# One kernel of sparse attention and an ELU layer, with its order of work written anew: PSUM pairs in neighbouring banks, no clamps on GpSimd, tile fills between the loads

## The chip, the cores and the metric

The kernel runs on one core of a Trainium2 chip. The metric is device time in microseconds (us), the median of three runs. A core has five engines that are used here: TensorE (PE in the rows, PEld for its weight loads), VectorE (DVE), ScalarE (ACT), GpSimd (POOL, which also issues most loads) and SyncE (SP, which issues stores and transposing DMAs). They run side by side, each in its own fixed order, and wait for each other through semaphores. PSUM is the memory that TensorE writes its results to; it has 8 banks of 512 f32 columns.

## The reference

Eight heads of attention over 8 batches of 576 tokens, then a feed-forward layer with ELU:

```python
def _attn_ref(q, k, v):                       # (8, 8, 576, 64)
    scores = scale * np.matmul(q, k.transpose(0, 1, 3, 2))
    rel = pos[:, None] - pos[None, :]
    mask_local = (rel >= 0) & (rel < 32)                              # heads 0 to 3
    mask_strided = (rel >= 0) & (pos[None, :] % 32 == pos[:, None] % 32)   # heads 4 to 7
    attn = softmax(where(mask, scores, -1e9))
    return np.matmul(attn, v)

x = attn_out.transpose(0, 2, 1, 3).reshape(4608, 512)
h = x @ w_in                                  # 512 x 2048
g = np.where(h > 0.0, h, np.exp(np.minimum(h, 0.0)) - 1.0)
return g @ w_out                              # 2048 x 512
```

## The kernel before

The tokens of each batch are taken in 8 strided classes, so that a strided head attends inside its class pairs and a local head inside 32 neighbours. A piece of attention work is named `bcy.u`: batch `b`, kind `c` (`s` strided, `l` local), half `y` of the four heads, half `u` of the queries; there are 8 such pieces in a batch and 64 in all. A piece runs through a chain: scores `S` (TensorE, L418), exponential `e` (ScalarE, L425), mask `m` (VectorE, L432 or L438), times v and sums `O` (TensorE, L481 or L488; L445 to L466 in batches 0 and 1), logarithm of the sums `n` and its negative exponential `r` (ScalarE, L516 and L522: the reciprocal), and the product `x` that writes the layer's input `xT` (VectorE, L547).

The feed-forward layer takes the 4608 tokens in 9 chunks of 512. For each chunk 16 blocks `L` (or `a` and `b`, its two halves) of 4 matmuls make h (L595), ScalarE exponentiates (`h`, L603), a clamp to `exp(h) - 1` at most 0 follows (`i` on VectorE, `j` on ScalarE, `p` on GpSimd: L612 and L610), and VectorE takes the maximum with h into `g` (`g`, L623). Then 16 parts `Z` of 4 matmuls (L629) make the output, four parts to each 128 rows, which ScalarE copies out of PSUM (`o`, L635) and SyncE stores (`t`, L647).

All PSUM is one tile `ps` of 8 banks. A token of the text `ORDER` names the banks it writes: `L.1.3.1` one bank, `S.2s0.0.27` a pair, here banks 2 and 7. A pair is read in one instruction, as a slice with a step:

```python
def banks(s):
    i, j = int(s[0]), int(s[1])
    return ps[:, i:j + 1:j - i, 0:W]
```

The order of all work is that text: the loop at the end calls a function for each token, and so each engine gets its instructions in the order of the tokens. The layer below it sets the semaphore waits from the tiles and slices that instructions read and write.

Batches 0 and 1 are transposed by TensorE (`T`, L382 and L385). From batch 2 on, GpSimd loads q, k and v (`Ls`, `Ll`: L238, L245, L252, L262, L264), SyncE transposes them by DMA (`Ts`, `Tl`: L574, L577, L580) and copies the keys into zero-padded tiles `kps` and `kpl` (`Ks`, `Kl`: L588). The 8 spare rows of the tiles that are transposed are filled once from q (L563), inside `load_str` of batch 2. The padded tiles and the constant blocks of the v tiles are filled by GpSimd (L325 to L333), after all loads of the list `LOADS`. A run of `w` tokens is TensorE multiplying zeros (L363).

Of the kernel before, what the change touches and what calls it, by code (L numbers as in the profile page):

```python
# [46 lines left out]
n.0l0.0 m.0l1.0 O.0l1.1.67 r.0l0.0 n.0l0.1 O.0l1.0.23 x.0l0.0 r.0l0.1 a.0.0.0 n.0l1.0 x.0l0.1
a.0.1.1 r.0l1.0 a.0.2.4 n.0l1.1 x.0l1.0 a.0.3.5 r.0l1.1 a.0.4.2 x.0l1.1 a.0.5.3 b.0.0 b.0.1
h.0.0 b.0.2 h.0.1 b.0.3 i.0.0 g.0.0 b.0.4 h.0.3 b.0.5 i.0.1 h.0.4 a.0.6.6 i.0.3 g.0.1 b.0.6
h.0.5 a.0.7.7 g.0.3 h.0.2 b.0.7 j.0.5 a.0.8.0 i.0.2 i.0.4 a.0.9.1 h.0.6 g.0.4 b.0.8 h.0.7 g.0.5  # L50
a.0.10.5 j.0.7 a.0.11.2 g.0.2 a.0.12.3 h.0.8 g.0.7 b.0.9 j.0.6 b.0.10 i.0.8 h.0.9 g.0.6 b.0.11
h.0.10 b.0.12 g.0.8 a.0.13.4 h.0.12 i.0.10 a.0.14.7 g.0.10 h.0.11 Ll.2 b.0.13 b.0.14 i.0.12
# [60 lines left out]
L.5.2.4 i.5.0 h.5.1 g.5.0 O.6s0.0.15 i.5.1 h.5.2 L.5.3.2 g.5.1 n.6s0.0 i.5.2 L.5.4.7 r.6s0.0
g.5.2 Kl.6 Ll.7 O.6s0.1.03 h.5.3 x.6s0.0 Z.4.0.3.6 n.6s0.1 i.5.3 S.6s1.0.14 g.5.3 r.6s0.1
# [43 lines left out]
def kernel(  # L158
# [162 lines left out]
    for nm in LOADS:  # L321
        load(nm)
# [374 lines left out]
```

## Time and profile before

| | |
|---|---|
| three runs | 404.1, 404.48, 406.24 us, median 404.48 |
| the profiled execution | 405.33 us, of which the span is 403.4 |
| busy share of PE, DVE, ACT, POOL | 79%, 59%, 57%, 26% |
| mean granted TensorE clock | 0.961 of full speed |
| DMA moved | 40.59 MB, mean 101 GB/s |

The span is cut in stages by what TensorE does: until 20.6 us the attention of batch 0; until 80 the layer's chunk 0, the attention of batch 1 and the first loads for batch 2; until 332 the attention of batches 2 to 7, with blocks `L` and parts `Z` between; and from there the rest of the layer alone. The views give busy times per engine, and for idle time the instruction whose end released the one that waited.

### The profile page before, as it was taken

To read this page: it belongs to the slowest core of one execution; us is meant where nothing else is said; L and a number is where in the kernel's file an instruction comes from. 1 tells how busy PE (TensorE), PEld (TensorE's weight loads), DVE (VectorE), ACT (ScalarE), POOL (GpSimd) and SP (SyncE) were. 2 spreads that over 40 slices of the span, in tenths; PEclk is the share of its full clock that TensorE was granted. 3 is DMA by queue.
4 is the path that set the end of the run, shared out by engine and by line. 5 is a ranking of instruction groups with operands and counts; after the bars stand their busy time and mean duration, and the time that the engine had idled before them with its cause. 6 is when DMAs were issued, how large, how long until landed. Compare 5 with 4: busy or idle time off the path is not lost.

```text
span 403.4 us, 6126 instructions
## 1 busy us (share of the span) xinstructions
PE 319.4 (79%) x2263; PEld 161.2 (40%) x2302; DVE 237.0 (59%) x431; ACT 228.0 (57%) x388; POOL 106.2 (26%) x135
## 2 busy tenths in 40 slices
PE   6896788675778777778577686878988789999995
PEld 5643434332334343344233343434444334444442
DVE  3779835366416866665447665777467649639300
ACT  3785464464546775657556565676667756346121
POOL 8639932155000670432361205200000000000000
PEclk9999598899958999999999999999999999999999
DMA  8999996959714894898199819931421110110132
GB/s 151 189 206 189 132 159 130 156 63 175 117 26 120 125 132 80 137 150 143 49 117 134 165 41 144 83 89 51 99 72 28 26 28 0 48 58 0 53 80 79
DMA packets 110214, 40.59 MB, mean 101 GB/s; under 512 B 91784, under 2 KB 103752, under 8 KB 110184
## 3 DMA queue, kind: packets, MB, share of 16 engines
q0 software_dynamic: 71376, 18.75, 46.6%
q1 hardware_dynamic: 38808, 21.44, 22.8%
q8 instruction: 18, 0.29, 0.3%
q14 instruction: 12, 0.10, 0.1%
HBM read 38.03 MB, written 9.44 MB: 118 GB/s over the span
## 4 chain that ended last, share of the span: by engine, by line
PE 52%; DVE 18%; ACT 15%; DMA 8%; issue 4%; POOL 2%; SPq 0%; ACTq 0%; DVEq 0%; POOLq 0%
PE ps L629 24%; PE ps L595 21%; DVE xT L547 7%; ACT ln L516 6%; DVE g L623 5%; DVE he L612 5%; ACT e L425 4%; PE ps L418 4%; ACT he L603 2%; DMA kl<-in_k_dram 2%; ACT rc L522 2%; DMA kps<-kTs 2%; DMA qTs<-qs 2%; DMA ks<-in_k_dram 1%; PE ps L488 1%
## 5 line engine op out<-in xcount | busy, mean ns | idle before, releaser
L629 PE MATMUL ps<-w_out_sb,g 128*128 128x512 bf16 x557 | 143.6, 390 | 20.5 <-DVE xT L547 8.6
L595 PE MATMUL ps<-xT,w_in_sb 128*128 128x512 bf16 x556 | 137.5, 383 | 16.5 <-DVE xT L547 6.3
L603 ACT ACTIVATE he<-ps 128x512 f32<-128x512 f32 x144 | 84.4, 597 | 46.7 <-PE ps L595 36.0
L623 DVE TENSOR_TENSOR g<-he,ps 128x512 bf16<-128x512 bf16 x136 | 93.2, 687 | 21.7 <-ACT ln L516 7.3
L629 PEld LDWEIGHTS <-g 128*128 128x128 bf16 x576 | 54.4, 100 | 81.9 <-issue 30.7
L595 PEld LDWEIGHTS <-w_in_sb 128*128 128x128 bf16 x576 | 54.8, 98 | 79.7 <-issue 22.8
L612 DVE TENSOR_SCALAR he<-he 128x512 bf16<-128x512 f32 x130 | 64.0, 494 | 29.8 <-ACT he L603 29.4
L547 DVE TENSOR_TENSOR xT<-ps,rc 64x576 bf16<-64x576 f32 (+1 forms) x64 | 43.4, 680 | 62.9 <-ACT e L425 15.8
L425 ACT ACTIVATE e<-ps 72x576 bf16<-72x576 f32 (+1 forms) x64 | 40.9, 647 | 33.5 <-PE ps L418 13.7
L516 ACT ACTIVATE ln<-ps 64x576 f32<-64x576 f32 (+1 forms) x64 | 37.4, 584 | 38.0 <-PE ps L629 10.7
L635 ACT COPY osb<-ps 128x512 f32<-128x512 f32 x36 | 21.1, 585 | 40.1 <-PE ps L629 36.5
L522 ACT ACTIVATE rc<-ln 64x576 f32<-64x576 f32 (+1 forms) x64 | 39.7, 621 | 2.0
L245 POOL DMA_DIRECT2D ql<-in_q_dram x24 | 20.1, 845 | 46.5 <-DMA qTl<-ql 46.5
L612 POOL TENSOR_SCALAR he<-he 128x512 bf16<-128x512 f32 x6 | 12.0, 2004 | 48.8 <-ACT he L603 48.8
L418 PE MATMUL ps<-qTs,kps 128*128 128x72 bf16 x192 | 10.6, 198 | 15.7 <-DVE xT L547 5.7
L252 POOL DMA_DIRECT2D kl<-in_k_dram x24 | 18.1, 786 | 0.0
L432 DVE TENSOR_TENSOR pm<-e,mask_s 72x576 bf16<-72x576 bf16 x32 | 14.5, 461 | 5.9 <-ACT e L425 5.3
L438 DVE TENSOR_TENSOR pm<-e,mask_l 128x576 bf16<-128x576 bf16 x32 | 14.4, 454 | 5.9 <-ACT e L425 5.2
L418 PEld LDWEIGHTS <-kps 128*128 128x128 bf16 x192 | 9.1, 99 | 21.6 <-issue 18.8
L481 PE MATMUL ps<-pm,vsp 72*128 72x72 bf16 x192 | 11.0, 201 | 5.2 <-DVE xT L547 1.6
L481 PEld LDWEIGHTS <-vsp 72*128 72x128 bf16 x192 | 9.9, 101 | 12.6 <-issue 7.4
L418 PE MATMUL ps<-qTl,kpl 128*128 128x96 bf16 x144 | 10.3, 211 | 5.4 <-ACT ln L516 4.1
(87 smaller groups left out, 174.1 us busy)
## 6 DMA issues: line engine op xcount, KB each, us to landing
out_dram<-osb SPq DMA_DIRECT2D x32, 144.0 KB
vl<-in_v_dram POOLq DMA_DIRECT2D x8, 288.0 KB, 6.5
w_in_sb<-in_moe_w_in_dram POOLq DMA_DIRECT2D x4, 512.0 KB, 10.3
w_out_sb<-in_moe_w_out_dram POOLq DMA_DIRECT2D x4, 512.0 KB, 14.8
vs<-in_v_dram POOLq DMA_DIRECT2D x7, 288.0 KB, 7.7
kps<-kTs SPq DMA_DIRECT2D x12, 160.0 KB
ql<-in_q_dram POOLq DMA_DIRECT2D x24, 72.0 KB, 3.5
kl<-in_k_dram POOLq DMA_DIRECT2D x24, 72.0 KB, 3.7
```

The costliest lines, as they stand in the source:

```text
L418: nc.tensor.matmul(dst, lhsT=kt[pr, k0:k0 + 128], rhs=rhs, start=True, stop=True, skip_group_check=True)
L425: nc.scalar.activation(e[0:R], tiles.pop(("S", key, u))[0:R], ACT.Exp, scale=scale)
L481: nc.tensor.matmul(ov[:, x, j * RS:(j + 1) * RS], lhsT=vs_p[:, c0:c0 + 128], rhs=pm[0:RS, z, n0:n0 + RS], start=True, stop=True, skip_grou ...
L516: nc.scalar.activation(t, s_ps, ACT.Ln)
L522: nc.scalar.activation(t, tiles.pop(("ln", key, u)), ACT.Exp, scale=-1.0)
L547: nc.vector.tensor_mul(dst, o_ps, rc)
L595: nc.tensor.matmul(tiles["h", ch, m], lhsT=w_in_sb[:, c, m * 128:(m + 1) * 128], rhs=xT[:, c, ch * CHUNK:(ch + 1) * CHUNK], start=(c == 2) ...
L603: nc.scalar.activation(e, tiles["h", i[0], i[1]], ACT.Exp)
L612: eng.tensor_scalar(e1, e, scalar1=1.0, scalar2=1.0, op0=ALU.min, op1=ALU.subtract)
L623: nc.vector.tensor_tensor(dst, e1, h, op=ALU.max)
L629: nc.tensor.matmul(ops, lhsT=g[ch % 2][:, m, kk * 128:(kk + 1) * 128], rhs=w_out_sb[:, m, :], start=(m == 0), stop=(m == MC - 1), skip_gro ...
L635: nc.scalar.copy(o_sb, tiles.pop(("o", int(ch), int(kk))))
```

## The change

There are four edits. Every token of `ORDER` is placed anew, and its pairs are now all neighbours (01, 12, ... 67); the code that reads them is unchanged. The new text has no `p` token: the 6 clamps on GpSimd are gone, `j` has 9 in place of 8, and VectorE has 135 clamps in place of 130. There are 68 zero matmuls `w` in place of 30. The fills of padded tiles and constant blocks are cut in seven, and one stands after each load from the fifth of `LOADS` on. The fill of spare rows moves out of `load_str` of batch 2 to a place after the load `wi3`, ahead of `wo0`.

```diff
 ORDER = """
-w.7.28 K.q.1 K.q.0 K.k.1 K.k.0 T.0s0.q.0 c.0s0.q T.0s0.k.1 T.0s1.q.2 c.0s0.k T.0s1.k.3 C.0s1.q
...
+w.7.42 K.q.0 K.q.1 T.0s0.q.0 K.k.0 w.7.5 C.0s0.q T.0s1.q.1 K.k.1 w.7.2 T.0s1.k.0 C.0s1.q w.7.1
...
-    for nm in LOADS:
-        load(nm)
-
-    for (c, z), t in kp.items():
+    def fill_kp(c, z):
+        t = kp[c, z]
         nc.gpsimd.memset(t[(1 - z) * D:(2 - z) * D, :], 0.0)
-        if c == "s":
-            nc.gpsimd.memset(t[z * D:(z + 1) * D, 2 * NS * RP:], 0.0)
-        else:
-            nc.gpsimd.memset(t[z * D:(z + 1) * D, 0:PRE], 0.0)
-    for t, n in ((vl_t[0], HG * LB), (vl_t[1], HG * LB), (vs_p, HG * NS)):
+        s_ = slice(2 * NS * RP, None) if c == "s" else slice(0, PRE)
+        nc.gpsimd.memset(t[z * D:(z + 1) * D, s_], 0.0)
+
+    def fill_ones(t, n):
         nc.gpsimd.memset(
             t[:, 0:2 * n * D].rearrange("p (n w d) -> p n w d", w=2, d=D)[:, :, 0, :], 1.0)
         nc.gpsimd.memset(t[:, 2 * n * D:], 1.0)
+
+    def fill_rows(nm, x):
+
+        nc.gpsimd.dma_start(
+            out=raw[nm][RS:RP].rearrange("p (h f) -> p h f", h=HG),
+            in_=x[0, 0:HG].rearrange("h (p s) d -> p h (s d)", s=NS)[0:RP - RS])
+
+    fills = [lambda cz=cz: fill_kp(*cz) for cz in kp]
+    fills += [lambda a=a: fill_ones(*a)
+              for a in ((vl_t[0], HG * LB), (vl_t[1], HG * LB), (vs_p, HG * NS))]
+    for i, nm in enumerate(LOADS):
+        load(nm)
+        if nm == "wi3":
+            for a in (("qs", q), ("ks", k), ("ql", q)):
+                fill_rows(*a)
+        elif i >= 4 and fills:
+            fills.pop(0)()
...
-        if int(b) == NPE:
-
-            for nm, x in (("qs", q), ("ks", k), ("ql", q)):
-                nc.gpsimd.dma_start(
-                    out=raw[nm][RS:RP].rearrange("p (h f) -> p h f", h=HG),
-                    in_=x[0, 0:HG].rearrange("h (p s) d -> p h (s d)", s=NS)[0:RP - RS])
```

Lines of the changed kernel that stand behind the text are named by its own numbers: `L` and `Z` are L603 and L637 there, `e`, `n`, `r` and `x` L439, L530, L536 and L561, and `h`, `o` L611 and L643.

The first place is GpSimd's queue in the load stage, ahead of the loads of batch 2 (`ql` and `kl` in the last rows). Before:

```order
L325 MEMSET kpl_109 64x1184
L329 MEMSET kpl_109 64x32
L331 MEMSET vl_99 128x24x64
L333 MEMSET vl_99 128x64
L331 MEMSET vl_100 128x24x64
L333 MEMSET vl_100 128x64
L331 MEMSET vsp 72x32x64
L333 MEMSET vsp 72x64
L245 DMA ql<-in_q_dram 72x8x64 x4
L252 DMA kl<-in_k_dram 96x6x64 x4
```

And now:

```order
L238 DMA g_88<-in_v_dram 72x4x512
L328 MEMSET vl_99 128x24x64
L330 MEMSET vl_99 128x64
L238 DMA xT<-in_q_dram 72x4x512
L328 MEMSET vl_100 128x24x64
L330 MEMSET vl_100 128x64
L238 DMA xT<-in_k_dram 72x4x512
L328 MEMSET vsp 72x32x64
L330 MEMSET vsp 72x64
L262 DMA vl_100<-in_v_dram 96x24x64
L275 DMA w_out_sb<-in_moe_w_out_dram 128x4x512 x2
L245 DMA ql<-in_q_dram 72x8x64 x4
```

The fourteen memsets of the seven fills no longer stand in one run between the last load of `LOADS` and the first of batch 2; at most two follow each other.

The second place is ScalarE's queue where batch 2 ends and batch 3 begins (`ln<-ps` twice is `n` of the pieces 2l1.0 and 2l1.1, in banks 1 and 5, and 3 and 6), with the semaphores that each row waits for. Before:

```order
L425 ACTIVATE e<-ps 128x576 [waits DVE_49,PE_49]
L425 ACTIVATE e<-ps 128x576 [waits DVE_49]
L635 COPY osb<-ps 128x512 [waits DMAHW5_49,DMAHW4_49,DMAHW3_49]
L425 ACTIVATE e<-ps 72x576 [waits DVE_49,PE_49]
L516 ACTIVATE ln<-ps 64x576 [waits PE_49] x2
L522 ACTIVATE rc<-ln 64x576 [waits Activation_49]
L522 ACTIVATE rc<-ln 64x576
L425 ACTIVATE e<-ps 72x576 [waits DVE_49]
```

And now, where the first `ln` is that of 2l1.1, in banks 3 and 4, and the second that of 2l1.0, in banks 0 and 1:

```order
L439 ACTIVATE e<-ps 128x576 [waits DVE_49,PE_49]
L536 ACTIVATE rc<-ln 64x576 [waits Activation_49]
L439 ACTIVATE e<-ps 72x576 [waits DVE_49,PE_49]
L530 ACTIVATE ln<-ps 64x576 [waits DVE_49]
L530 ACTIVATE ln<-ps 64x576 [waits PE_49,Activation_49]
L536 ACTIVATE rc<-ln 64x576 [waits Activation_49]
L536 ACTIVATE rc<-ln 64x576 [waits DVE_49]
L439 ACTIVATE e<-ps 72x576 [waits PE_49]
L643 COPY osb<-ps 128x512 [waits DMAHW7_49,DMAHW6_49,DMAHW5_49]
```

The work is nearly the same and in nearly the same order; what moved is which banks the waits are about. In the built program of before, the first of the two `ln` waits for part `Z.1.1.1.4` and the second for `Z.1.1.2.4`, both in bank 4, which neither reads; now the first waits for an earlier VectorE reader of its own bank 4, and the second for the matmuls into its own bank 1. Followed in this way through both built programs, from each wait's value to the instruction that raises the semaphore to it, 668 waits of before tie two instructions that both touch PSUM with a bank in common or with one lying between the other's two, and in 276 of them no bank is common; of those 276, 85 are waits of PE, 121 of ACT and 70 of DVE. In the changed program there are 671 such waits and every one has a bank in common. PE's own waits of this sort were 133 with a common bank and 85 without, and are now 238 and none.

The third place is GpSimd's queue in the middle of the program, where clamps stood ahead of the loads of a batch:

```order
-L612 TENSOR_SCALAR he_1611<-he 128x512
-L245 DMA ql<-in_q_dram 72x8x64 x4
-L252 DMA kl<-in_k_dram 96x6x64 x4
-L262 DMA vl_99<-in_v_dram 96x24x64
-L264 DMA vl_99<-in_v_dram 32x23x64
-L612 TENSOR_SCALAR he_1762<-he 128x512
```

The loads stay, in the same order among themselves; no clamp stands between them.

## Rows read from the trace of the kernel before

**Rows 1.** The page, part 1: busy time of the engines.
```profile
PE 319.4 (79%) x2263; PEld 161.2 (40%) x2302; DVE 237.0 (59%) x431; ACT 228.0 (57%) x388; POOL 106.2 (26%) x135
```
**Rows 2.** Stages: length; busy PE, PEld, DVE, ACT, POOL; PE's clock; DMA; GB/s.
```profile
0.00:20.60 20.60, 15.22 (x254) 12.74 (x255) 11.50 (x31) 12.26 (x24) 15.71 (x30) 1.00 1.16 171
20.60:80.00 59.40, 46.29 (x390) 23.72 (x397) 37.92 (x63) 33.37 (x66) 30.33 (x39) 0.86 1.24 163
80.00:332.00 252.00, 191.34 (x1318) 94.63 (x1342) 154.67 (x273) 156.25 (x256) 60.11 (x67) 0.97 0.69 96
332.00:403.40 71.40, 66.56 (x304) 30.14 (x308) 32.96 (x64) 26.14 (x44) 0.00 (x0) 1.00 0.16 45
```
**Rows 3.** What PE waited for: total us, times, longest.
```profile
PE ps L418 <- ACT ln L516: 9.5, 9, 2.0
PE ps L629 <- DVE xT L547: 8.6, 7, 2.1
PE ps L629 <- ACT e L425: 6.4, 9, 0.9
PE ps L595 <- DVE xT L547: 6.3, 8, 1.2
PE ps L418 <- DVE xT L547: 5.7, 5, 2.0
...
PE ps L595 <- ACT e L425: 4.3, 5, 1.1
PE ps L595 <- ACT ln L516: 4.2, 6, 1.5
PE ps L629 <- ACT ln L516: 3.7, 5, 0.7
```
**Rows 4.** Timeline, 113 to 122 us: start, length, instruction, idle time before it.
```profile
113.28 1.86 PE L629 MATMUL ps<-w_out_sb,g 128*128 128x512 bf16 x4 [0.73 <-ACT e L425]
115.18 0.64 ACT L516 ACTIVATE ln<-ps 64x576 f32<-64x576 f32 x1 [1.95 <-PE ps L629]
...
118.25 0.64 ACT L516 ACTIVATE ln<-ps 64x576 f32<-64x576 f32 x1 [2.43 <-PE ps L629]
...
118.94 3.57 PE L629 MATMUL ps<-w_out_sb,g 128*128 128x512 bf16 x8 [0.73 <-ACT ln L516]
...
120.92 1.44 DVE L547 TENSOR_TENSOR xT<-ps,rc 64x576 bf16<-64x576 f32 x2 [7.20 <-ACT e L425]
```
**Rows 5.** Timeline, 36.9 to 42.8 us: a clamp beside GpSimd's fills.
```profile
36.91 5.02 DVE L612 TENSOR_SCALAR he<-he 128x512 bf16<-128x512 f32 x1
...
36.95 1.38 POOL L331 MEMSET vl<- 128x1536 bf16 x1
...
39.76 1.80 POOL L331 MEMSET vsp<- 72x2048 bf16 x1
...
42.71 0.64 PE L382 MATMUL ps<-identity,xT 72*128 72x72 bf16 x8 [4.63 <-DVE g L623]
```
**Rows 6.** The same columns, after that stall and around rows 4.
```profile
42.70:51.00 8.30, 7.74 (x112) 4.97 (x113) 7.21 (x15) 5.14 (x10) 8.30 (x11) 0.50 1.53 110
110.00:125.00 15.00, 11.19 (x68) 5.11 (x67) 3.92 (x7) 7.35 (x12) 0.00 (x0) 0.66 0.18 38
```
**Rows 7.** Timeline, batch 2's loads: last row fill, first transpose, first scores.
```profile
53.05 0.64 POOL L563 DMA_DIRECT2D ql<-in_q_dram  x1
...
61.14 1.39 SPq L574 DMA_TRANSPOSE qTs<-qs  x1
...
74.07 0.19 PE L418 MATMUL ps<-qTs,kps 128*128 128x72 bf16 x1 [2.77 <-DMA kps<-kTs]
```
**Rows 8.** Groups by line: clamps on both engines, and the zero matmuls.
```profile
L612 DVE TENSOR_SCALAR he<-he 128x512 bf16<-128x512 f32 x130 | 64.0, 494 | 29.8 <-ACT he L603 29.4
L612 POOL TENSOR_SCALAR he<-he 128x512 bf16<-128x512 f32 x6 | 12.0, 2004 | 48.8 <-ACT he L603 48.8
L363 PE MATMUL ps<-zero 128*128 128x128 bf16 x30 | 3.8, 312 | 1.1 <-DVE zero L289 1.1
```

More of the change, by code (lines that the diff above doesn't have):

```diff
@@ L47 @@
[L47 to L52, printed above, removed]
@@ new lines @@
+S.0s1.1.23 T.0l0.q.4 e.0s1.0 m.0s0.1 e.0s1.1 O.0s0.0.56 c.0l0.q O.0s0.1.01 m.0s1.1 n.0s0.0
+T.0l1.q.7 m.0s1.0 r.0s0.0 n.0s0.1 x.0s0.0 T.0l0.k.4 r.0s0.1 C.0l1.q O.0s1.0.23 c.0l0.k
+O.0s1.1.56 n.0s1.0 x.0s0.1 T.0l1.k.7 r.0s1.0 V.0 n.0s1.1 S.0l0.0.01 x.0s1.0 r.0s1.1 w.4.2
+c.0l1.k e.0l0.0 S.0l0.1.23 w.4.4 x.0s1.1 e.0l0.1 m.0l0.0 S.0l1.1.01 S.0l1.0.45 m.0l0.1 e.0l1.1
+O.0l0.0.67 e.0l1.0 O.0l0.1.23 m.0l1.1 a.0.0.0 n.0l0.0 m.0l1.0 O.0l1.1.45 r.0l0.0 n.0l0.1 a.0.1.1
+x.0l0.0 r.0l0.1 O.0l1.0.67 n.0l1.1 x.0l0.1 r.0l1.1 a.0.2.2 n.0l1.0 x.0l1.1 a.0.3.3 r.0l1.0
@@ new lines @@
+T.1l0.q.3 i.0.15 g.0.15 S.1s0.0.12 i.0.14 T.1l1.q.5 e.1s0.0 g.0.14 T.1l0.k.7 c.1s1.k C.1l1.q
+c.1l0.q S.1s0.1.12 m.1s0.0 S.1s1.1.45 c.1l0.k e.1s0.1 T.1l1.k.3 e.1s1.1 m.1s0.1 O.1s0.0.12 V.1
+S.1s1.0.67 n.1s0.0 c.1l1.k O.1s0.1.45 e.1s1.0 m.1s1.1 Z.0.0.1.0 n.1s0.1 m.1s1.0 r.1s0.1
+O.1s1.1.67 r.1s0.0 x.1s0.1 Z.0.0.2.0 n.1s1.1 x.1s0.0 r.1s1.1 O.1s1.0.34 x.1s1.1 S.1l0.0.12
+n.1s1.0 Z.0.0.3.0 r.1s1.0 e.1l0.0 x.1s1.0 S.1l0.1.56 o.0.0 S.1l1.0.34 m.1l0.0 Z.0.1.0.7 e.1l0.1
+t.0.0 e.1l1.0 m.1l0.1 O.1l0.0.12 S.1l1.1.56 m.1l1.0 n.1l0.0 O.1l0.1.34 Ll.2 r.1l0.0 Ls.2
@@ new lines @@
+Z.0.3.0.3 e.2s0.1 x.2s0.0 e.2s1.0 m.2s0.1 S.2s1.1.45 Z.0.3.1.3 Ts.3 e.2s1.1 m.2s1.0 h.1.9
+O.2s0.1.12 m.2s1.1 O.2s1.0.67 L.1.10.4 n.2s0.1 i.1.9 g.1.9 r.2s0.1 Z.0.3.2.3 n.2s1.0 x.2s0.1
+Z.0.3.3.3 r.2s1.0 h.1.10 O.2s1.1.01 x.2s1.0 L.1.11.2 n.2s1.1 i.1.10 S.2l0.0.56 g.1.10 r.2s1.1
+L.1.12.7 e.2l0.0 x.2s1.1 L.1.13.4 Ks.3 o.0.3 m.2l0.0 h.1.11 W.3 S.2l0.1.56 O.2l0.0.01 t.0.3
+h.1.12 i.1.11 L.1.14.3 Ls.4 g.1.11 n.2l0.0 i.1.12 r.2l0.0 L.1.15.2 g.1.12 h.1.14 x.2l0.0
+Z.1.0.0.7 h.1.13 i.1.14 e.2l0.1 g.1.14 S.2l1.1.01 Z.1.0.1.7 e.2l1.1 m.2l0.1 i.1.13 h.1.15
@@ new lines @@
+m.2l1.1 O.2l0.1.56 S.2l1.0.01 g.1.13 n.2l0.1 Z.1.0.2.7 Tl.3 i.1.15 e.2l1.0 g.1.15 O.2l1.1.34
+r.2l0.1 m.2l1.0 S.3s0.0.01 Z.1.0.3.7 e.3s0.0 x.2l0.1 n.2l1.1 m.3s0.0 O.2l1.0.01 S.3s1.0.56
+n.2l1.0 Z.1.1.0.2 r.2l1.0 Z.1.1.1.2 r.2l1.1 x.2l1.0 Z.1.1.2.2 e.3s1.0 x.2l1.1 o.1.0 O.3s0.0.01
+m.3s1.0 n.3s0.0 Kl.3 Ll.4 L.2.0.3 r.3s0.0 L.2.1.7 t.1.0 h.2.0 x.3s0.0 L.2.2.4 h.2.1 i.2.0 g.2.0
+S.3s0.1.56 h.2.2 O.3s1.0.01 i.2.1 L.2.3.3 e.3s0.1 i.2.2 g.2.2 n.3s1.0 L.2.4.5 g.2.1 h.2.3
+L.2.5.4 m.3s0.1 h.2.4 i.2.3 r.3s1.0 O.3s0.1.67 i.2.4 Z.1.1.3.2 g.2.3 n.3s0.1 g.2.4 L.2.6.3
@@ new lines @@
+S.7s1.0.45 i.6.3 L.6.4.6 e.7s1.0 g.6.3 O.7s0.1.12 m.7s1.0 h.6.4 Z.5.0.2.7 n.7s0.1 i.6.4
+O.7s1.0.34 g.6.4 L.6.5.0 r.7s0.1 n.7s1.0 x.7s0.1 S.7s1.1.56 Z.5.0.3.7 r.7s1.0 e.7s1.1 L.6.6.1
+x.7s1.0 h.6.5 m.7s1.1 S.7l0.0.56 Z.5.1.0.4 o.5.0 i.6.5 g.6.5 h.6.6 t.5.0 O.7s1.1.23 L.6.7.7
+e.7l0.0 i.6.6 g.6.6 n.7s1.1 S.7l0.1.56 m.7l0.0 Z.5.1.1.4 r.7s1.1 h.6.7 O.7l0.0.01 x.7s1.1
+Z.5.1.2.4 n.7l0.0 i.6.7 g.6.7 L.6.8.2 r.7l0.0 e.7l0.1 x.7l0.0 L.6.9.7 h.6.8 m.7l0.1 S.7l1.0.56
+h.6.9 i.6.8 O.7l0.1.01 g.6.8 e.7l1.0 L.6.10.3 i.6.9 n.7l0.1 g.6.9 Z.5.1.3.4 r.7l0.1 m.7l1.0
@@ new lines @@
+L.8.4.0 h.8.3 i.8.2 g.8.2 L.8.5.1 h.8.4 i.8.3 g.8.3 L.8.6.7 h.8.5 i.8.4 g.8.4 L.8.7.2 h.8.6
+i.8.5 L.8.8.0 g.8.5 h.8.7 i.8.6 L.8.9.3 g.8.6 h.8.8 i.8.7 L.8.10.1 h.8.9 g.8.7 L.8.11.7 i.8.8
+h.8.10 g.8.8 L.8.12.2 i.8.9 h.8.11 g.8.9 L.8.13.0 h.8.12 i.8.10 g.8.10 L.8.14.3 h.8.13 i.8.11
+g.8.11 L.8.15.1 h.8.14 i.8.12 Z.7.0.1.6 g.8.12 h.8.15 i.8.13 Z.7.0.2.6 g.8.13 i.8.14 Z.7.0.3.6
+g.8.14 i.8.15 Z.7.1.0.0 o.7.0 g.8.15 Z.7.1.1.0 t.7.0 Z.7.1.2.0 Z.7.1.3.0 Z.7.2.0.1 o.7.1
+Z.7.2.1.1 t.7.1 Z.7.2.2.1 Z.7.2.3.1 Z.7.3.0.0 o.7.2 Z.7.3.1.0 t.7.2 Z.7.3.2.0 Z.7.3.3.0
@@ L154 @@
+Z.8.0.0.1 o.7.3 Z.8.0.1.1 t.7.3 Z.8.0.2.1 Z.8.0.3.1 Z.8.1.0.0 o.8.0 Z.8.1.1.0 t.8.0 Z.8.1.2.0
+Z.8.1.3.0 Z.8.2.0.1 o.8.1 Z.8.2.1.1 t.8.1 Z.8.2.2.1 Z.8.2.3.1 Z.8.3.0.0 o.8.2 Z.8.3.1.0 t.8.2
+Z.8.3.2.0 Z.8.3.3.0 o.8.3 t.8.3
 """
```

179 lines of the change are left out of this document (73 added, 106 removed).

## The prediction

> **What bounds the kernel now.** The first view is the busy time of the engines [rows 1]: PE is the busiest at 319.4 us of a span of 403.4, so 84.0 us of the span are PE idle, and no other engine is over 59%. The span therefore ends where PE's work plus PE's idle time ends, and what I look for is what ended each idle stretch. The second view cuts the busy time by stage [rows 2]. Before 20.6 us PE idles 5.4, until 80 us 13.1, in the attention of batches 2 to 7 60.7, and in the rest 4.8. So nearly three quarters of the idle time lie in the third stage, where VectorE and ScalarE are busy 61% and 62% of it: nobody is full, and everybody waits. The same rows show a clock loss: at 0.86 in the second stage and 0.97 in the third, about 46.29 x 0.14 = 6.5 and 191.34 x 0.03 = 5.7 us of PE's time were lost to the lower of the two clock levels, 1.2 instead of 2.4 GHz.
>
> The third view is PE's waits [rows 3]. The eight longest that concern this change sum to 48.7 us, and they are odd: output parts (L629) and blocks of the first layer (L595) wait for an exponential, a logarithm or a write of `xT` in attention, with which they share no data. The fourth view is a timeline of one such place [rows 4]: a part L629 waits 0.73 us for `e`; then `ln` waits 1.95 for that part; the next `ln` waits 2.43 for the next part; PE waits 0.73 for that `ln`; `xT` sits idle 7.20. Two streams that share nothing run in turns instead of side by side. In the program these are the waits without a common bank that the second order excerpt shows: a pair with a step is treated as if it took all banks from its first to its last. The timeline gives their price, the program only their place.
>
> **Part by part.** The sum is made against the profiled execution, 405.3 us, which is 0.85 above the median of the three runs.
>
> Neighbouring pairs and the new order (term 1). All 276 waits without a common bank go. What of PE's idle time was theirs? I take each of the eight rows [rows 3] with the share of the program's waits between those two lines that have no common bank: L418 behind `ln` 9 of 12 of 9.5, L629 behind `xT` 8 of 8 of 8.6, L629 behind `e` 11 of 13 of 6.4, L595 behind `xT` 8 of 17 of 6.3, L418 behind `xT` 5 of 16 of 5.7, L595 behind `e` 9 of 12 of 4.3, L595 behind `ln` 7 of 12 of 4.2, L629 behind `ln` 7 of 7 of 3.7. That is 7.1 + 8.6 + 5.4 + 3.0 + 1.8 + 3.2 + 2.4 + 3.7 = 35.2 us, the upper bound. It is not all won, since behind each stands a true wait: PE has 105 more waits on a common bank than before (238 against 133), because neighbours must be free together and pairs such as 0 and 1 are used again at once. In before, 218 waits of PE on PSUM cost the 48.7 us, 0.22 each; 105 x 0.22 = 23 us would leave a gain of 12. But a part of that 0.22 was handed on: ScalarE and VectorE were themselves held by 191 waits of this kind, as the 1.95, 2.43 and 7.20 us show [rows 4]. I take half of the upper bound, **-17.6** (0.17 per new wait), and keep -35 and +10 as the ends; a loss cannot be excluded, as the rivals say.
>
> Fills between the loads (term 2). In before a clamp on VectorE, 0.49 us in the mean [rows 8], took 5.02 us, exactly while GpSimd ran its last six memsets back to back, and PE then sat 4.63 us [rows 5]. Cut in pieces of at most 1.80 us [rows 5] and parted by loads, the fills can no longer hold VectorE for so long; but they now stand earlier, and I work out from the order that four of the seven still meet the clamps of chunk 0. Between 0 and -4.6 I take **-3.0**, nearer the latter since the stall is a measured row. The Trainium skill, "SBUF — State Buffer", section "SBUF: two separate sides", says that VectorE in a two-port mode and GpSimd exclude each other, and that who starts first holds the shared ports for its whole instruction. By that rule alone the clamp would have waited for one memset, at most 1.80 us; the trace shows 5.02, so it does not agree on the length. By it the four fills could each hold a clamp again for their whole length, the term would be 0, and the time 378.
>
> Clock (term 3). After the 4.63 us of idleness PE ran 8.3 us at a granted clock of 0.50, and around rows 4 it ran 15 us at 0.66 [rows 6]: 7.74 x 0.50 = 3.9 and 11.19 x 0.34 = 3.8 us of slow work. Both follow from idle time that terms 1 and 2 remove. I take **-6.0**, ends 0 and -12 (all that is lost in rows 2).
>
> Row fills ahead of `wo0` (term 4). The last of the three was issued at 53.05, the first transpose of batch 2 could start at 61.14 only, and PE's first scores of batch 2 came at 74.07 after 2.77 us of waiting for the padded keys [rows 7]. Now no row fill follows batch 2's loads (3 x 0.64 us of issue), and GpSimd reaches those loads earlier. But the DMA engines move 163 GB/s over that stage with a share over 1 [rows 2], so the data comes little sooner. **-2.0**, ends 0 and -5. GpSimd's queue pays three issues earlier instead, with the loads of batch 1 behind them: 3 x 0.64 = 1.9 us at a point where its loads wait for the DMA engines anyway, so nothing; were that cover gone, 1.9.
>
> No clamps on GpSimd (term 5). One took 2004 ns, on VectorE 494 [rows 8], and GpSimd waited 48.8 us for their inputs with loads queued behind. Those loads were not late later on, so that wait costs nothing. Five more clamps add 5 x 0.49 = 2.5 us to VectorE, hidden in its 41% of idle time. The six chains shorten by 1.5 us each, of which I count one on the path: **-1.5**, ends -9 and +2.5.
>
> Zero matmuls (term 6). 38 more at 3.8 / 30 = 0.127 us [rows 8] are 4.8 us at most. They stand before the layer's first block, where PE idles 5.4 of 20.6 us. **+0.5**, ends 0 and 4.8.
>
> Stage four stays: PE is busy 66.56 of 71.4 us there [rows 2]; more or less work behind attention only shifts between stages.
>
> Sum: 405.3 - 17.6 - 3.0 - 6.0 - 2.0 - 1.5 + 0.5 = 375.7, against the median 374.9; I say **375**.
>
> **The rivals.**
> - *Nearly everything comes back.* If the new order is met as written, term 1 gives its whole 35, the clock 9, the rest -7: 405 - 51 = 354, with 5 more or less. For it speaks that VectorE and ScalarE have 38% of idle time in the third stage; against it, that PE's waits on PSUM grow in number, from 218 to 238.
> - *The waits move.* The 105 new waits cost the old 0.22 to 0.30 each: term 1 is -12 to -4, the clock gives 3, the fills 1, the rest 1: about 391, between 386 and 402. For it speaks that the order still has TensorE wait in line behind a reader of the bank that it writes next.
> - *Slower.* One mechanism: PE is blocked in order by a pair that isn't free. A block or part behind such a score waits too, though its own bank is free. The place is the third stage, where scores and `O` follow each other in the same pair. The price is 105 x p; the other terms without the clock are -6, so it decides from p = (35.2 + 6) / 105 = 0.39 us on, and at p = 0.45 the idle time that stays also keeps the clock low: 405 + 6 = 411. The longest single waits of that kind took 2.0 us [rows 3]; against it stands the mean of 0.22.
> - *No change that can be told.* The pace is set by loads, not by waits on PSUM: then 404. Against it: PE waited for padded keys 2.77 us at the first scores [rows 7], and no DMA is among the long rows of PE's waits [rows 3].
>
> **How the numbers follow.** The forecast (363 to 386) gets 0.54, nearly everything 0.15, the moved waits 0.19, slower 0.08, no change 0.04. So faster by over 0.5% (2 us, about what a measurement of this kernel can tell from no change) has 0.54 + 0.15 + 0.19 = 0.88, the same 0.04, slower 0.08. The range from 357 to 397 leaves out the lower part of the second case (some 0.09) and, above, the tail of the third, no change and slower (some 0.13 in all).
>
> **What would show it.** In the changed profile PE's rows for L603 and L637 (the old L595 and L629) should have hardly any idle time behind `e`, `ln` and `xT`; what stays should stand at L432, L495 and L502. No clamp should take 5 us; the clock should be 1.00 from 42 to 51 us; PE's idle time in the stage of batches 2 to 7 should fall from 61 to some 40 us. I am wrong if that idle time stays at 55 or more with new releasers on the same banks, or if the first scores of batch 2 come later than 74 us.

## The result and the profile after

The changed kernel takes 337.48 us (median of 4 runs, 334.4 to 340.7) beside 404.88 for the kernel before on the same chip: a ratio of 0.831, 95% interval 0.824 to 0.838. Measured again it took 337.01 (6 runs, ratio 0.832, 0.828 to 0.836). Ratios and intervals, here and below, are taken from fast runs alone and medians from all; of the first four the 340.7 counts as slow. The forecast was 375, the range 357 to 397: the sign was right, and the gain was more than twice the one forecast. The profiled execution took 334.4, of which the span is 332.7. First the busy times of the page, to read beside [rows 1]:

```profile
PE 307.2 (92%) x2301; PEld 158.5 (48%) x2340; DVE 233.6 (70%) x434; ACT 226.7 (68%) x391; POOL 95.0 (29%) x129
```

PE's idle time fell from 84.0 to 25.5 us, and its busy time by 12.2, though 38 zero matmuls more are in it. Together that is the whole difference of the spans, 403.4 - 332.7 = 70.7. The stages, in the columns of [rows 2]; the attention of batches 2 to 7 now ends near 250 us, so the third is cut at 255, and the fifth row is the stretch that the prediction named:

```profile
0.00:20.60 20.60, 16.19 (x287) 13.28 (x288) 9.97 (x29) 14.12 (x28) 18.10 (x34) 0.83 1.17 171
20.60:80.00 59.40, 51.63 (x461) 26.07 (x468) 45.39 (x80) 40.40 (x76) 30.53 (x40) 0.94 1.34 174
80.00:255.00 175.00, 167.59 (x1238) 87.47 (x1261) 145.24 (x263) 145.45 (x244) 46.42 (x57) 0.99 1.03 132
255.00:332.70 77.70, 71.78 (x319) 31.64 (x324) 32.96 (x64) 26.74 (x45) 0.00 (x0) 0.98 0.17 47
42.00:51.00 9.00, 7.75 (x136) 4.52 (x136) 7.82 (x18) 6.30 (x13) 5.68 (x7) 0.81 1.72 145
```

The time came from the third stage: 175 us in place of 252, with 7.4 us of PE idle in place of 60.7. VectorE and ScalarE are busy 83% there, up from 61% and 62%: nearly the same work, closer together. A part of the 77 us only moved, since PE is busy 5.3 us more in the second stage and 5.2 more in the last. What PE waited for, beside [rows 3]:

```profile
PE ps L432 <- DMA kps<-kTs: 5.6, 4, 3.7
PE ps L603 <- DVE g L629: 2.9, 1, 2.9
PE ps L603 <- DVE g L631: 2.9, 7, 1.0
...
PE ps L432 <- ACT e L439: 0.5, 1, 0.5
...
PE ps L432 <- DVE xT L561: 0.4, 2, 0.2
```

Seven of the eight rows of [rows 3] are gone, the eighth (scores behind `xT`, now L432) is 0.4 us, and all that stands behind `e`, `ln` and `xT` is 0.9 us, where all such rows of before are 61.3. The readers tell why. These are the groups of the three instructions that read pairs, before, with the idle time of their engine ahead of them and what ended it:

```profile
L547 DVE TENSOR_TENSOR xT<-ps,rc 64x576 bf16<-64x576 f32 (+1 forms) x64 | 43.4, 680 | 62.9 <-ACT e L425 15.8 <-PE ps L629 14.8 <-ACT rc L522 12.8
L425 ACT ACTIVATE e<-ps 72x576 bf16<-72x576 f32 (+1 forms) x64 | 40.9, 647 | 33.5 <-PE ps L418 13.7 <-PE ps L629 6.1 <-PE ps L595 5.0
L516 ACT ACTIVATE ln<-ps 64x576 f32<-64x576 f32 (+1 forms) x64 | 37.4, 584 | 38.0 <-PE ps L629 10.7 <-DVE g L623 7.0 <-PE ps L595 5.4
```

and the same three after:

```profile
L561 DVE TENSOR_TENSOR xT<-ps,rc 64x576 bf16<-64x576 f32 (+1 forms) x64 | 43.3, 679 | 20.5 <-ACT rc L536 19.5
L439 ACT ACTIVATE e<-ps 72x576 bf16<-72x576 f32 (+1 forms) x64 | 40.6, 646 | 11.3 <-PE ps L432 10.4 <-DVE pm L452 0.3
L530 ACT ACTIVATE ln<-ps 64x576 f32<-64x576 f32 (+1 forms) x64 | 37.4, 584 | 7.2 <-PE ps L459 2.3 <-PE ps L495 1.8 <-PE ps L502 1.6
```

One instruction takes the same time to 1 ns (680 and 679, 647 and 646, 584 and 584): two banks with a gap are read as fast as two neighbours. (In the groups of `xT` and `ln`, 16 of the 64, in batches 0 and 1, read one bank. The forms that read pairs take 755 and 754, 644 and 645 ns alone, and 755 and 644 in after's order with all pairs apart, a run below.) What went is 95 us of idle time ahead of them (134.4 to 39.0), and with it the wrong releasers: layer matmuls (L629, L595) that have nothing to do with what is read. What is left are nearly all true producers.

### The profile page after: what moved, and what is told of

Read it like the earlier page. It is cut to its first block, busy times and chain, and to the rows that moved or that the text cites. A ratio compares the mean times of both kernels' runs of the same rounds, so it can differ in the third digit from the quotient of the medians.

```text
span 332.7 us, 6226 instructions
## 1 busy us (share of the span) xinstructions
PE 307.2 (92%) x2301; PEld 158.5 (48%) x2340; DVE 233.6 (70%) x434; ACT 226.7 (68%) x391; POOL 95.0 (29%) x129
## 4 chain that ended last, share of the span: by engine, by line
PE 62%; DVE 18%; DMA 10%; issue 3%; ACT 3%; POOL 1%; SPq 1%; another core or an unknown queue 0%; DVEq 0%; ACTq 0%
PE ps L637 33%; PE ps L603 21%; DVE g L631 8%; DVE he L620 6%; DMA kTs<-ks 4%; PE ps L432 4%; DMA kps<-kTs 3%; DMA kl<-in_k_dram 3%; DVE xT L561 2%; PE ps L502 2%; PE ps L495 1%; ACT e L439 1%; ACT he L611 1%; ACT ln L530 1%; DVE g L629 1%
## 5 line engine op out<-in xcount | busy, mean ns | idle before, releaser
L603 PE MATMUL ps<-xT,w_in_sb 128*128 128x512 bf16 x557 | 140.1, 382 | 7.8 <-DVE g L629 2.9
L637 PE MATMUL ps<-w_out_sb,g 128*128 128x512 bf16 x556 | 137.6, 383 | 1.6 <-DVE g L631 0.2
L611 ACT ACTIVATE he<-ps 128x512 f32<-128x512 f32 x144 | 84.5, 597 | 37.2 <-PE ps L603 31.7
L603 PEld LDWEIGHTS <-w_in_sb 128*128 128x128 bf16 x576 | 54.3, 98 | 70.2 <-issue 13.8
L620 DVE TENSOR_SCALAR he<-he 128x512 bf16<-128x512 f32 x135 | 64.2, 477 | 25.0 <-ACT he L611 24.5
L637 PEld LDWEIGHTS <-g 128*128 128x128 bf16 x576 | 53.5, 99 | 58.3 <-issue 4.0
L561 DVE TENSOR_TENSOR xT<-ps,rc 64x576 bf16<-64x576 f32 (+1 forms) x64 | 43.3, 679 | 20.5 <-ACT rc L536 19.5
L439 ACT ACTIVATE e<-ps 72x576 bf16<-72x576 f32 (+1 forms) x64 | 40.6, 646 | 11.3 <-PE ps L432 10.4
L643 ACT COPY osb<-ps 128x512 f32<-128x512 f32 x36 | 21.0, 584 | 39.3 <-PE ps L637 36.4
L530 ACT ACTIVATE ln<-ps 64x576 f32<-64x576 f32 (+1 forms) x64 | 37.4, 584 | 7.2 <-PE ps L459 2.3
L536 ACT ACTIVATE rc<-ln 64x576 f32<-64x576 f32 (+1 forms) x64 | 39.6, 621 | 1.9
L432 PE MATMUL ps<-qTs,kps 128*128 128x72 bf16 x192 | 10.9, 200 | 5.8 <-DMA kps<-kTs 5.6
L432 PEld LDWEIGHTS <-kps 128*128 128x128 bf16 x192 | 9.4, 100 | 11.7 <-DMA kps<-kTs 4.4
L238 POOL DMA_DIRECT2D qs<-in_q_dram x7 | 5.3, 764 | 33.5 <-DMA qTs<-qs 33.4
L495 PEld LDWEIGHTS <-vsp 72*128 72x128 bf16 x192 | 9.1, 98 | 5.3 <-issue 0.7
L502 PEld LDWEIGHTS <-vl 128*128 128x128 bf16 x144 | 8.9, 98 | 5.4 <-issue 0.8
L432 PEld LDWEIGHTS <-kpl 128*128 128x128 bf16 x144 | 8.3, 97 | 4.7 <-DMA kpl<-kTl 0.8
```

What stands on the lines that cost most here:

```text
L432: nc.tensor.matmul(dst, lhsT=kt[pr, k0:k0 + 128], rhs=rhs, start=True, stop=True, skip_group_check=True)
L439: nc.scalar.activation(e[0:R], tiles.pop(("S", key, u))[0:R], ACT.Exp, scale=scale)
L530: nc.scalar.activation(t, s_ps, ACT.Ln)
L536: nc.scalar.activation(t, tiles.pop(("ln", key, u)), ACT.Exp, scale=-1.0)
L561: nc.vector.tensor_mul(dst, o_ps, rc)
L603: nc.tensor.matmul(tiles["h", ch, m], lhsT=w_in_sb[:, c, m * 128:(m + 1) * 128], rhs=xT[:, c, ch * CHUNK:(ch + 1) * CHUNK], start=(c == 2) ...
```

## The experiments

### Bank numbers and the order, apart

The order of before, token for token, with its banks numbered anew so that all pairs are neighbours (381 of 1339 tokens change, in their digits alone):

```diff
-S.3s0.0.37 o.1.0 m.2l1.1 O.2l1.0.15 e.3s0.0 Z.1.1.1.4
+S.3s0.0.67 o.1.0 m.2l1.1 O.2l1.0.34 e.3s0.0 Z.1.1.1.2
```

> The order of before, token for token, with only the bank numbers chosen anew so that every pair is two neighbours (276 waits without a common bank become 0; banks are used again no sooner than before). Theory A, the waits without a common bank were the larger part of the 67 us: 350 to 375 us. Theory B, the order itself is what gained and these waits only stood beside other idle time: 395 to 405 us.

And the reverse, after's text with its bank numbers exchanged by one fixed permutation, so that neighbours are no longer neighbours:

```diff
-S.3s0.0.01 Z.1.0.3.7 e.3s0.0 x.2l0.1 n.2l1.1 m.3s0.0 O.2l1.0.01 S.3s1.0.56
+S.3s0.0.02 Z.1.0.3.4 e.3s0.0 x.2l0.1 n.2l1.1 m.3s0.0 O.2l1.0.02 S.3s1.0.16
```

> The changed kernel, token for token, with its eight banks renamed so that the pairs stand apart again (0 waits without a common bank become 251; which banks are free when is the same). Theory A: 375 us or more, PE idle again behind e, ln and xT. Theory B: under 350 us.

Measured: 343.88 (ratio 0.847, 0.841 to 0.853) and 384.22 (0.946, 0.940 to 0.952), before at 405.23. So digits alone give 61 us in the old order, and taking them back costs 47 in the new one. The exchange of numbers in the second run changes no instruction's work and not how soon a bank is used again, only who waits for whom. So it, more than the first run, shows the cause, since a new numbering of the old order also moves the true waits. The old order with neighbours, busy times and PE's waits:

```profile
PE 308.4 (90%) x2302; PEld 159.4 (47%) x2302; DVE 232.7 (68%) x431; ACT 225.1 (66%) x388; POOL 105.7 (31%) x135
```
```profile
PE ps L466 <- DVE xT L547: 5.2, 1, 5.2
PE ps L382 <- DVE g L623: 4.9, 2, 4.6
PE ps L418 <- DMA kps<-kTs: 4.7, 3, 2.4
...
PE ps L418 <- DVE xT L547: 1.4, 3, 0.9
```

Behind `e`, `ln` and `xT` 6.6 us are left; the second row is the stall of [rows 5], untouched. The first, 5.2 of the 6.6, is no wait of this kind either: that `xT` stood in VectorE's queue behind the copy of batch 2's strided v (`W`, L554), which waited for its load:

```profile
DVE vsp L554 <- DMA vs<-in_v_dram: 6.0, 1, 6.0
```

With after's order and pairs apart such waits are back, 45.0 us behind `e`, `ln` and `xT` in place of 0.9:

```profile
PE ps L637 <- DVE xT L561: 8.6, 12, 1.4
PE ps L603 <- DVE g L631: 5.9, 7, 3.6
PE ps L432 <- ACT e L439: 5.1, 7, 1.1
PE ps L637 <- ACT e L439: 4.7, 6, 1.2
```

### The fills alone

Before with the fills and row fills of after, and after with the old ones: of the diff above, the part below `ORDER` alone, put in and taken back.

```diff
-    for nm in LOADS:
-        load(nm)
...
+    for i, nm in enumerate(LOADS):
+        load(nm)
+        if nm == "wi3":
...
+        elif i >= 4 and fills:
+            fills.pop(0)()
```

> The kernel before with only the fills and row fills moved between the loads. As predicted (terms 2, 4 and half of 3): 396 to 400 us, the clamp of 5 us gone. Rival, the load stage is paced by the DMA engines: 403 to 405 us.

> The changed kernel with fills and row fills put back to where they stood. Theory A and the prediction's terms 2, 4: 342 to 348 us, with a clamp on VectorE of about 5 us. Rival, in the new order they don't matter: 336 to 339 us.

Measured: 399.98 (0.987, 0.980 to 0.994) and 341.72 (0.842, 0.837 to 0.847). The fills are worth 5.3 us in before (2 to 8 by the interval) and 4.2 in after, where this interval and after's just touch. The 21 us between before and after's order with pairs apart hold these 5.3, so the order with its clamps and zero matmuls gave 15.8 there (399.98 to 384.22).

The clamp of 5 us, expected to be gone, was not. In before with the new fills two clamps take 5.56 us beside the fills, and PE waits for the maximum behind them as long as it did, 5.0 us in place of 4.6:

```profile
28.06 5.56 DVE L620 TENSOR_SCALAR he<-he 128x512 bf16<-128x512 f32 x2
```
```profile
PE ps L603 <- DVE g L631: 5.0, 1, 5.0
```

What came sooner is batch 2. Its first transpose starts at 56.89 us in place of 61.14 and its first scores at 70.98 in place of 74.07, and PE's 3.1 us of waiting for padded keys are gone. The loads of its q are issued at the same time (49.80 us in before, 49.89); what is gone is the three row fills behind them. In after's order with the old fills the first scores come at 76.41, with the new ones at 69.19, and the wait for padded keys is longer by 4.0 us than after's 5.6, nearly the whole 4.2:

```profile
PE ps L418 <- DMA kps<-kTs: 9.6, 5, 6.0
```

### Which waits are dear

In the program, before has 276 waits on a bank that lies between: 85 of TensorE, 121 of ScalarE, 70 of VectorE. Two more numberings of the old order each keep mainly one kind. The first has 5, 111 and 42:

```diff
-S.3s0.0.37 o.1.0 m.2l1.1 O.2l1.0.15 e.3s0.0 Z.1.1.1.4
+S.3s0.0.47 o.1.0 m.2l1.1 O.2l1.0.56 e.3s0.0 Z.1.1.1.1
```

> The order of before, token for token, with banks numbered so that TensorE has nearly no wait on a bank that only lies between (5 of before's 85), while ScalarE keeps 111 of 121 and VectorE 42 of 70. The same order with neighbours took 343.9. Theory 1 (the readers' waits are the dear ones: they delay the exponentials and products for which TensorE then truly waits): 365 to 395. Rival, the bound of the prediction (what can come back is what TensorE itself waits for behind pair readers): no wait of that kind is left on TensorE, so 344 to 349.

The second has 78, 64 and 23, and no reader but one waits on a matmul between (the expectation says two):

```diff
-S.3s0.0.37 o.1.0 m.2l1.1 O.2l1.0.15 e.3s0.0 Z.1.1.1.4
+S.3s0.0.56 o.1.0 m.2l1.1 O.2l1.0.02 e.3s0.0 Z.1.1.1.7
```

> The order of before with banks numbered the other way: TensorE has 78 of its 85 waits on banks between, ScalarE and VectorE wait on no matmul between (2 in place of 74), though 86 of their waits on each other (of 117) stay. The neighbours took 343.9. Bound of the prediction (35.2 us of direct waits of TensorE times 78/85): 344 plus up to 32, so 360 to 376. Theory 1 with the readers' waits on matmuls as the only dear ones: 344 to 355. If both kinds count, 365 to 385.

Measured: 362.25 (0.891, 0.885 to 0.897) and 363.01 (0.890, 0.882 to 0.898), 18 and 19 us over the neighbours. The first sits a little under what the first theory asked for (365) and far over its rival's 344 to 349: with next to no such wait on TensorE the readers' waits cost 18 us all the same. (This numbering also gives 23 banks out again within 3 tokens of their last reader, neighbours 7. How much of the 18 that is was not tried apart; after does so 20 times, and a numbering of after with later reuse, below, gains 2 to 3 us.) In its rows ScalarE waits for layer matmuls:

```profile
ACT e L425 <- PE ps L595: 9.2, 11, 2.2
ACT e L425 <- PE ps L629: 8.8, 11, 1.7
ACT ln L516 <- PE ps L595: 8.0, 11, 1.4
```

and PE pays for it where it waits truly, on a reader of its own bank or a product that comes late:

```profile
PE ps L595 <- DVE g L623: 4.7, 5, 1.7
...
PE ps L595 <- ACT e L425: 3.2, 4, 1.0
PE ps L481 <- DVE pm L432: 3.2, 8, 1.2
PE ps L418 <- ACT e L425: 3.0, 5, 1.0
PE ps L418 <- DVE xT L547: 2.9, 4, 1.0
```

The second has the direct waits instead (its L595 waits 12.4 us behind `xT`, 13 times), and lies within the 360 to 376 of the prediction's bound; with "both count" put at 365 or more, that reading missed by 2 us, and the one that took the readers' waits on matmuls alone as dear (344 to 355) by 8. Both numberings together have more waits of the kind (158 + 165) than before, and cost 37.5 us in sum, where before's 276 cost 61. So the two kinds seem to cost more together than apart. That is a reading, not a proof: a new numbering moves each wait to another place.

### Is the order worth anything, once pairs are neighbours?

The old order in neighbouring banks with the new fills, and its `p` tokens (GpSimd) made `i` (VectorE):

```diff
-Z.0.2.3.2 p.1.2 h.1.3
+Z.0.2.3.2 i.1.2 h.1.3
```

> The order of before in neighbouring banks, with the fills of after and all clamps of GpSimd put on VectorE: what is left to after is the order alone. Theory 1 (bank numbers are nearly all, the order and the other edits a few us): neighbours 343.9, less 4 to 5 for the fills as measured in both orders, less 0 to 2 for the clamps: 337 to 341, after being at 337.5. Rival (the new order is worth what it gave with pairs apart, 404 to 384): 343 or more, with after 6 or more ahead.

> The changed kernel again, to stand beside the next three on the same chip: 336 to 339. No theory differs here.

> The order of before in neighbouring banks with all other edits, again. If the order written anew is worth nothing once no reader waits on a bank between (most of its gain with pairs apart was fewer of those waits): 334 to 338, within 1% of after. If it costs: 3 us or more below after. If it gives: 3 us or more above.

Measured: 334.86 (0.822, 0.816 to 0.828) at first; then, side by side on one chip, after 337.01 (0.832, 0.828 to 0.836) and the old order 336.65 (0.829, 0.826 to 0.833). The order written anew gives and costs nothing that can be measured. A bank numbering of after that reuses banks later (132 of 452 uses less than 8 tokens after the last reader, not 247) is the other half of that question:

```diff
-m.3s0.0 O.2l1.0.01 S.3s1.0.56 n.2l1.0 Z.1.1.0.2
+m.3s0.0 O.2l1.0.45 S.3s1.0.01 n.2l1.0 Z.1.1.0.6
```

> The order of after with its banks numbered anew, still all pairs neighbours, so that a bank is given out later after its last reader: 132 of 452 uses follow within 8 steps of the order, in place of 247. After is at 337.5. If the true waits on the same bank that stand in place of the others cost next to nothing, as after's rows say (waits of L603 and L637 behind e, ln and xT under 2 us together): 336 to 339. If they cost (the rival of the prediction, 0.1 us or more for each of the 105 new ones, of which perhaps half go here): 332 or less.

Measured: 334.61 (0.825, 0.821 to 0.829), 2 to 3 us under after with intervals that just overlap, and between the two ranges of the expectation. If waits on the same bank cost anything in after, it is about that.

### The small edits

After with one run of 30 zero matmuls, the other six `w` tokens left out; and, of the old order in neighbouring banks with the old fills, only `p` made `i`:

```diff
-w.7.42 K.q.0 K.q.1 T.0s0.q.0 K.k.0 w.7.5
+w.7.30 K.q.0 K.q.1 T.0s0.q.0 K.k.0
...
-Z.0.2.3.2 p.1.2 h.1.3
+Z.0.2.3.2 i.1.2 h.1.3
```

> After with 30 zero matmuls at the start in place of 68 in seven runs. If they only fill time in which TensorE waits for the first loads (price 0.5 us in the prediction): 336 to 338.5. If the later runs hold the granted clock up through the attention of batch 0 (after had 0.83 there and 0.94 from 20.6 to 80 us): 340 to 345, with a lower clock in the first 80 us. If they stand in the way: 333 to 335.5.

> The order of before in neighbouring banks with old fills, the 6 clamps of GpSimd put on VectorE and nothing else. The neighbours alone took 343.9, with the new fills as well 334.9: 9 us for two edits, of which the fills alone gave 4 to 5 in two other settings. If the two add up: 339 to 340. Prediction's term (1.5 us): 342 to 343. If a GpSimd clamp holds up the maximum behind it and so TensorE (VectorE had 6.3 us of idle behind them in the neighbours' trace): 337 to 340.

Measured: 336.99 (0.832, 0.827 to 0.837), so the 38 zero matmuls are worth nothing that can be measured. And 338.73 (0.836, 0.831 to 0.841): the clamps off GpSimd give some 5 us (against 343.88, 0.841 to 0.853, with before at 405.66 and 405.23 beside the two; the intervals just touch). In the old order with neighbours VectorE's maximum waited for them, and once PE did:

```profile
DVE g L623 <- POOL he L612: 6.3, 5, 2.7
```
```profile
PE ps L418 <- POOL he L612: 1.2, 1, 1.2
```

Last, the long clamp. In after it was not gone. The timeline at 30 us (start, length):

```profile
29.57 1.40 POOL L328 MEMSET vl<- 128x1536 bf16 x1
...
30.47 3.41 DVE L620 TENSOR_SCALAR he<-he 128x512 bf16<-128x512 f32 x1
30.89 0.17 POOL L330 MEMSET vl<- 128x64 bf16 x1
30.98 0.71 POOL L238 DMA_DIRECT2D xT<-in_k_dram  x1
...
31.68 1.82 POOL L328 MEMSET vsp<- 72x2048 bf16 x1
33.42 0.17 POOL L330 MEMSET vsp<- 72x64 bf16 x1
...
35.25 2.71 PE L603 MATMUL ps<-xT,w_in_sb 128*128 128x512 bf16 x8 [2.92 <-DVE g L629]
```

The maximum behind that clamp (L629) then held PE for 2.92 us. So the eight fills of key tiles went to VectorE, ahead of its first casts, and the three of ones to the first places between GpSimd's loads; in after's order, in the old order with all other edits (twice), and in after's order with later reuse:

```diff
-        nc.gpsimd.memset(t[(1 - z) * D:(2 - z) * D, :], 0.0)
+        nc.vector.memset(t[(1 - z) * D:(2 - z) * D, :], 0.0)
...
-    fills = [lambda cz=cz: fill_kp(*cz) for cz in kp]
-    fills += [lambda a=a: fill_ones(*a)
+    for cz in kp:
+        fill_kp(*cz)
+    fills = [lambda a=a: fill_ones(*a)
```

> After, with the eight fills of the padded key tiles on VectorE ahead of its first casts and the three fills of ones on GpSimd behind its first loads. In after a clamp on VectorE beside fills on GpSimd still takes 3.41 us, and others 1.39 and 0.99. If GpSimd's fills stretch VectorE's clamps and TensorE waits for that: no clamp over 0.7 us from 20 to 35 us, and 333 to 336. Rival (the stretch is hidden, and the fills cost VectorE its time in the head): 337 to 341.

> The order of before in neighbouring banks with all other edits (334.9), and the fills of the key tiles on VectorE ahead of its casts. In the order of after this took the long clamp away and changed nothing (337.3 against 337.5). The run without it still shows 5.9 us of clamps at 28 us. If the clamp's stretch holds TensorE up there (TensorE waits 4.9 us behind the maximum that follows it): 330 to 333. If the work in the head costs as much, as in after's order: 334 to 337.

> The same with the fills of the key tiles on VectorE ahead of its casts. If its 332.6 was the clamp's stretch that went: 331 to 334, 2 us or more under the run before. If it was chance: within 1 us of that run.

> The order of after with its banks numbered for later reuse (334.6) and the fills of the key tiles on VectorE (337.3 alone). If the two are small gains that add up: 332 to 334.5. If both were chance: 336 to 338.

Measured: in after's order no clamp there is over 0.65 us any more, and the time is 337.28 (0.828, 0.819 to 0.837), the same. Why nothing came of it stands further on in VectorE's queue, at the copy of batch 2's v, in after and with the fills on VectorE:

```profile
60.89 0.69 DVE L568 COPY vsp<-vs 72x2048 bf16<-72x2048 bf16 x1 [0.74 <-DMA vs<-in_v_dram]
```
```profile
60.89 0.69 DVE L569 COPY vsp<-vs 72x2048 bf16<-72x2048 bf16 x1 [3.73 <-DMA vs<-in_v_dram]
```

VectorE came there 3 us sooner and waited 3 us longer for the load. In the 14 of 18 traces in which the copy waits for its load it starts between 60.6 and 64.2 us, in before at 60.83. So the load sets the time of this place, and a stall of VectorE ahead of it is hidden there as far as the wait goes.

In the old order the time is 332.57 (0.822, 0.817 to 0.826), and again 333.50 (0.824, 0.820 to 0.827) beside 336.65 without it, by intervals that overlap a little. There the same copy waits 9.47 us, and without the edit 3.10, so why this order gains stays open. After's order with later reuse and these fills took 334.45 (0.826, 0.822 to 0.829). The old order with neighbours, no GpSimd clamps and these fills is the fastest of all, some 3.5 us or 1% under after, at the edge of what the intervals separate.

## Why the prediction missed

**Term 1, neighbouring pairs (-17.6, at most -35.2)**, is the step that failed. Numbering alone gave -61 where this term and **term 3 (clock, -6)** had -23.6. The old order with neighbours lost 51.2 us of PE's idle time and 11.0 of its busy time. Three choices made term 1 small:
- The bound counted only the part of each row [rows 3] that the program's direct waits without a common bank could hold, 35.2 of 48.7. The true waits in the same rows went too. They were true only in that PE needed a bank or a product; that it was late came at least in part from the readers' 191 waits. The run with nearly the readers' waits alone speaks for this: 18 us with 5 such waits left on PE. Those waits were in the prediction ("a part of that 0.22 was handed on"), as a reason to soften a discount; they should have raised the bound.
- The eight rows were the longest; further rows of the same kind brought PE's waits behind `e`, `ln` and `xT` to 61.3 us. Neighbours left 6.6 of them, 5.2 of it behind a load.
- The discount of half, for 105 new waits on a common bank at 0.17 us, has no ground in the rows: such waits behind `e` and `xT` take 0.9 us in after, 0.01 for each of the 105. With the 6.0 us behind `g` counted too, 2.9 of them behind the long clamp, it is 0.03 for each of PE's 238. A wait for a reader that is on time is a wait in the program and cost next to nothing here.

The price of 0.22 per wait divided the eight rows by all 218 waits; by [rows 3] only 54 stops made up the 48.7 us. It was a mean over waits that, as the readers' rows suggest, fed each other, and no constant to be carried into a program without the others.

**Term 3** itself was about twice too large. Counted as the prediction counts it, the clock's loss fell from 12.2 us to 9.0 in after (16.19 x 0.17 + 51.63 x 0.06 + 167.59 x 0.01 + 71.78 x 0.02). Most of PE's lost busy time is something the prediction has no term for: added up by line, its groups of matmuls are busy 356.3 us in before and 354.1 with neighbours, but they overlap by 45.7 us in place of 36.9. PE stopped 24 times for another engine or a load, not 82 times, and so one group more often ran into the next. (The ends of matmuls are modelled in a profile, so these sums are rough.)

**Terms 2 and 4 (fills -3.0, row fills -2.0)** were right in sum, 5.3 and 4.2 against 5.0, and that was luck. Term 2 rested on the stall of [rows 5], and the stall stayed: 5.0 us on PE in before with the new fills, 2.9 in after, and taking it away there changed nothing. What was gained came by term 4's way, batch 2's keys sooner: its first scores stand at 69.2 us in after, not 74.07 [rows 7]. That makes the row fills the likely source, though the two edits were not tried apart. From 42 to 51 us the clock was 0.81, not the 1.00 that was named.

**Term 5 (clamps, -1.5)** was probably too small: 5.2 in the old order with neighbours, with intervals that just touch. I counted one chain of six on the path, and VectorE's maximum stood five times behind a GpSimd clamp there, for 6.3 us. That such a wait has less cover once PE hardly idles is likely, but was not tried in the kernel before. **Term 6 (+0.5)** was right: nothing.

**The rivals.** "Nearly everything comes back" (354) had the right mechanism and was still 17 us short, since it took the same 35.2 as its end. "The waits move" and "slower" rested on a price for the new waits, which is 0.01 to 0.03 us, not 0.22 or 0.39. "No change" fell with the first row of the result; a load does set the pace of one place, near 61 us, but not of the rest. What would have shown the prediction wrong was named for the slow side only; the third stage's idle time went to 7.4 us, not 40.

## What to carry to other kernels

When engines wait for each other without sharing data, don't bound the gain by the bottleneck engine's own wrong waits: look also at the idle time ahead of the other engines' wrongly held instructions, and at all waits on these, the true ones too, since the reader may be late for a wrong reason. Neither sum is the gain itself: ahead of the readers 83.5 us went by numbering alone (134.4 to 50.9), PE's waits behind them fell by 54.7, and the time by 61. A slice with a step that is guarded as one block is cheap to read and dear to wait for, so number the banks so that blocks hold nothing else before working on the order. A new wait in the program cost next to nothing here, since its releaser was on time. And before a stall is mended, look whether the engine only waits for a load a little later.

## What the runs showed that was not expected

- A clamp on VectorE that started during a GpSimd memset of 1.40 us ended only at 33.88 us, after three memsets more (0.17, 1.82 and 0.17 us) and a DMA issue of 0.71 us among them. In [rows 5] it was 5.02 us. The Trainium skill, "SBUF — State Buffer", section "SBUF: two separate sides", has whichever of VectorE and GpSimd starts first hold the shared ports for its whole instruction, while the other blocks. Read as one GpSimd instruction for each clamp, as in term 2, this does not agree with the trace: both stalls outlast one memset (spans on GpSimd are rough in a profile). Why the clamp did not get in between two of GpSimd's instructions stays open.
- The Trainium skill, "PSUM — Partial Sum Buffer", section "PSUM bank collisions raise a hardware error", asks for guards between engines on the same bank, and states that accesses to different banks run clean. By that the waits on a bank between guarded nothing, and the runs put their price at 61 us in this order; a pair apart without those waits was not tried.
- The granted clock of the first 20.6 us is not set by the kernel alone: one and the same kernel, the old order with all edits and VectorE's fills, had 0.69 in one profile and 1.00 in the other, with 332.63 and 334.37 us. In the eleven traces with 30 zero matmuls it was 1.00 six times and 0.68 or 0.69 five times, in the seven with 68 it was 0.83 to 0.86. What sets the clock so early stays open, and it cost nothing that shows.
